# Cutting the token tiles of a fused attention and two-layer kernel along the batches

## The chip, the cores and the metric

The kernel runs on one core of a Trainium2 chip. The metric is the device time of one execution in microseconds; lower is better.

## The reference

```python
def _attn_ref(q, k, v, f):                   # q, k, v: (8, 8, 576, 64); f: (8, 8, 576)
    scores = scale * np.matmul(q, k.transpose(0, 1, 3, 2))
    log_f = np.log(np.clip(f, 0.0001, 1.0))
    cum = np.cumsum(log_f, axis=-1)
    decay = cum[:, :, :, None] - cum[:, :, None, :]
    scores = np.where(causal, -1000000000.0, scores + decay)
    ...                                      # softmax
    return np.matmul(attn, v)
def _moe_ref(x, w_in, w_out):                # x: (4608, 512); w_in: (512, 2048)
    h = x @ w_in
    relu6 = np.clip(h + 3.0, 0.0, 6.0)
    g = h * relu6 / 6.0
    return g @ w_out
x = attn_out.transpose(0, 2, 1, 3).reshape(B * S, H * D)
```

Causal attention with a decay is computed for 8 batches of 8 heads, 576 positions each. Its output, 4608 rows of 512, goes through two dense layers with a hard swish between them.

## The kernel before

**Attention.** A list of 68 steps `v`: 4 of kind A and 8 of kind B make batch 0, and 56 of kind F (steps 12 to 67) are one head each of batches 1 to 7. A step F computes scores on TensorE (`pn`, two halves, lines 608 and 611), takes row maxima on VectorE (619), exponentials (631) and a 16-bit cast (645) on ScalarE, a remainder on VectorE or GpSimd (648, 654), turns the result by DMA transposes (`pT<-ring`, 666) and multiplies it with V (`pav`, lines 691 to 696). All operands of the two layers are split into two 16-bit parts, a high and a low one, so each product there is three matmuls.

**Hand-over.** When two heads are done, their 128 columns of `x` are split into `xhl`, and `x_move` (755) turns them by DMA transposes into `xT`, the tile buffer from which the first layer reads. These, like all transfers of the attention part, are issued on SP's queue. There are three `xT` buffers of 512 rows; buffer 2 also holds raw V of batch 0 at the start (`v0`).

**Two layers.** Rows are cut into 9 tiles of 512. Since a batch has 576 rows, tile `t` (1 to 7) holds the last `64 t` rows of batch `t-1` and the first `512 - 64 t` of batch `t`; its `x` comes in runs of 64 rows. `h_unit` makes 128 of the 2048 hidden columns for the tile: 12 matmuls into an accumulator `ph` (lines 781 to 783), a Relu on ScalarE for each batch in the tile (791, since the scale is per batch), a multiply on VectorE (794), a cast on ScalarE (795) and a subtraction on VectorE (796), which fill `gT`. `out_unit` makes 128 output rows: 48 matmuls (803 to 805), a scaled copy on ScalarE (814), one transfer out (815). A tile has 16 first-layer and 4 output units; tile 0 is done in two halves of 256 rows. Accumulators of both kinds rotate over three slots.

**Order.** The units of a tile are put in a list once the last heads of its batch are handed over, so tiles 7 and 8 after the last head. `fill` is called eight times a step; each call adds a rate to a credit, and units are emitted while there is credit: `H_COST` twice for a first-layer unit, some 64 in all for a tile. The rate is `F_RATE`: 0.6 for batch 0, 0.45 for batch 1, 1.02 after. From this emission order a scheduler sets, when the program is built, the fixed order of the instructions on each engine; a later instruction can pass an earlier one there that it expects to wait. On the chip each engine then runs its list in order.

Of the kernel before, what the change touches and what calls it, by code (L numbers as in the profile page):

```python
# [15 lines left out]
ALU = mybir.AluOpType  # L16
# [4 lines left out]
def kernel(  # L21
# [32 lines left out]
    cpool = ctx.enter_context(tc.tile_pool(name="cpool", bufs=1))  # L54
    p2 = ctx.enter_context(tc.tile_pool(name="p2", bufs=2))
# [22 lines left out]
        out=W[:, 4 * P:], in_=W[:, 4 * P:], pattern=[[-1, P]],  # L78
# [16 lines left out]
    QA = 256  # L95
    CA = QA // P
# [21 lines left out]
    def init_qk(i, eng):  # L118
# [11 lines left out]
    VR = H * (D + 1)  # L130
# [21 lines left out]
    SV, IV, UO, UX, A1 = 0, 8, 16, 24, 32  # L152
# [47 lines left out]
    def scol(c):  # L200
        return SC[:, c:c + 1]
# [172 lines left out]
    def moe_scale_in(b, j):  # L374
        nc.vector.scalar_tensor_tensor(
            scol(A1 + NG * b + j), scol(IV + b), CG, scol(I1 + j), op0=ALU.mult, op1=ALU.mult
        )

    def moe_scale_out(b):
        nc.vector.scalar_tensor_tensor(  # L380
            scol(UO + b), scol(IV + b), 1.0 / (6.0 * CG), scol(I1R), op0=ALU.mult, op1=ALU.mult
        )
# [195 lines left out]
    for half in NAT:  # L578
        g = [0]
# [3 lines left out]
    o = 0  # L583
# [155 lines left out]
    def x_move(v):  # L739

        kind, n = VH[v]
        g = n if kind == "A" else n // 2
        b, cc = divmod(g, NPAIR)
        xhl = xpair[g][1]
        c0, c1 = {"A": (0, CA), "B": (CA, NCH), "F": (0, NCH)}[kind]

        if kind == "F":
            runs = [(0, 0, 1, 0), (0, 1, NCH, 1), (64, 1, NCH, 2)]
        else:
            runs = [(r * 64, c0, min(c1, NCH - r), r + 2 * c0) for r in range(2)]  # L750
        for r, c, last, u in runs:
            while c < last:
                t, q = divmod(S // 64 * b + u, TT // 64)
                k = min(last - c, (TT // 64 - q + 1) // 2)
                nc.sync.dma_start_transpose(
                    xT[t % 3][:, cc, q % 2, q // 2:q // 2 + k].rearrange("p c a t -> p (c a) t"),
                    xhl[r:r + 64, c:c + k].rearrange("p c a e -> p (c a e)"),
                )
# [13 lines left out]
    def h_unit(t, fc, c0, c1):  # L772
        x = xT[t % 3]
        nw = c1 - c0
        ph = mm_tile(f"ph_{t}_{fc}_{c0}", t > 0 or c0 > 0)[:, :nw]
        fs_ = slice(fc * P, (fc + 1) * P)
        for cc in range(NCC):
            xh, xl = (
                x[:, cc, :, c0 // P:c1 // P, hl].rearrange("p h c t -> p c h t") for hl in range(2)
            )  # L780
            nc.tensor.matmul(ph, w1[0][:, cc, fs_], xh, start=(cc == 0), stop=False)  # L781
            nc.tensor.matmul(ph, w1[0][:, cc, fs_], xl, start=False, stop=False)  # L782
            nc.tensor.matmul(ph, w1[1][:, cc, fs_], xh, start=False, stop=(cc == NCC - 1))  # L783
            if cc == 1 and nw == TT:
                yield H_COST
        r = p2.tile([P, TT], F32, tag="rt", name=f"r_{t}_{fc}_{c0}", bufs=3)[:, :nw]
        segs = [(0, nw, min(t, B - 1))]
        if 0 < t < B:
            segs = [(0, 64 * t, t - 1), (64 * t, TT, t)]
        for a, e, b in segs:  # L790
            nc.scalar.activation(  # L791
                r[:, a:e], ph[:, a:e], AF.Relu, bias=bias_r, scale=scol(A1 + NG * b + fc * NG // NFC)
            )
        nc.vector.scalar_tensor_tensor(r, r, 6.0 * CG, ph, op0=ALU.min, op1=ALU.mult)  # L794
        nc.scalar.copy(gT[:, 0, fc, c0:c1], r)  # L795
        nc.vector.tensor_tensor(gT[:, 1, fc, c0:c1], r, gT[:, 0, fc, c0:c1], op=ALU.subtract)  # L796
        yield H_COST

    def out_unit(t, s):
        po = mm_tile(f"po_{t}_{s}", t > 0 or s * P >= QA)  # L800
        ts_ = slice(s * P, (s + 1) * P)
        for fc in range(NFC):
            nc.tensor.matmul(po, gT[:, 0, fc, ts_], w2[:, fc, 0, :], start=(fc == 0), stop=False)  # L803
            nc.tensor.matmul(po, gT[:, 0, fc, ts_], w2[:, fc, 1, :], start=False, stop=False)  # L804
            nc.tensor.matmul(po, gT[:, 1, fc, ts_], w2[:, fc, 0, :], start=False, stop=(fc == NFC - 1))  # L805
            if fc % 2 and fc < NFC - 1:
                yield 2.0 - H_COST
        g = t * 4 + s
        b = (g * P) // S
        col = UO + b  # L810
        if (g * P + P - 1) // S != b:
            col = UX + b + 1
        o = p2.tile([P, DM], F32, tag="o", name=f"o_{t}_{s}")
        nc.scalar.activation(o, po, AF.Copy, scale=scol(col))  # L814
        nc.sync.dma_start(out[g * P:(g + 1) * P, :], o)
# [61 lines left out]
    units = []  # L877
# [36 lines left out]
    for i, (kind, n) in enumerate(VH):  # L914
        b, h = divmod(n, H)
        if kind == "A":
            b = h = 0
        wn = W_RATE["ABF".index(kind)]
        rates[0] = F_RATE[0] if kind == "B" else F_RATE[min(b, 2)]
        ahead = i + 2 < NV  # L920
# [99 lines left out]
```

## Time and profile before

| | |
|---|---|
| median of 3 runs | 1087.07 us (1083.17 to 1088.06) |
| profiled execution | 1083.28 us, span 1081.5 us |
| mean granted TensorE clock | 0.982 of full speed |
| busy: TensorE, VectorE, ScalarE, GpSimd | 93%, 67%, 56%, 38% |
| HBM read, written | 47.93 MB, 9.73 MB |
| DMA engines busy | 54.7% by the main queue |
| `x` hand-over | 148 DMA transposes |

The span runs from the first to the last instruction of the program; the execution's own time is 1.8 us longer. Groups of instructions are named by line, engine, operation and tile, with the count behind an x, then busy us and mean ns of one, then the idle time just before them with the instruction that ended it. A matmul's duration includes its way through the array, so consecutive ones overlap, and what a stream costs is read from the distance of the starts.

### The profile page before, as it was taken

What the parts mean: (1) busy time and instruction counts of PE and PEld (TensorE: products, weight loads), DVE (VectorE), ACT (ScalarE), POOL (GpSimd) and SP (SyncE); (2) the same over time, 40 slices, a digit from 0 to 9 for tenths busy, and PEclk for the clock granted to TensorE, in tenths of its full rate; (3) what the DMA queues carried; (4) which work ended last, traced back from release to release, by engine and by line L of the source; (5) the groups of instructions that cost most, each with busy time, mean ns of one, the idle gap of its engine ahead of it and who ended that gap; (6) DMA issues with size and microseconds to landing.
All of it is one profiled execution on the core that took longest, in us unless ns stands there. A gap on an engine that the chain in (4) does not pass through costs nothing.

```text
span 1081.5 us, 20281 instructions
## 1 busy us (share of the span) xinstructions
PE 1010.1 (93%) x7074; PEld 577.4 (53%) x7074; DVE 719.7 (67%) x1887; ACT 610.1 (56%) x1285; POOL 413.1 (38%) x505
## 2 busy tenths in 40 slices
PE   2799977988999999999999989999999999999998
PEld 2567854755555555555555545555555555444443
DVE  7869899876885688468865795689668841510520
ACT  4778656845764577356754674477447841621520
POOL 7344455335434445444544444454445420000000
PEclk9989989999999999999999999999999999999999
DMA  8866547767756666667576856675666651000001
GB/s 258 277 172 194 150 105 134 179 127 150 156 114 141 140 146 118 137 129 164 108 139 138 164 113 130 146 166 114 128 140 128 106 112 46 1 10 30 1 1 39
DMA packets 261650, 133.74 MB, mean 124 GB/s; under 512 B 229444, under 2 KB 231036, under 8 KB 261548
## 3 DMA queue, kind: packets, MB, share of 16 engines
q1 hardware_dynamic: 261548, 132.45, 54.7%
q8 instruction: 56, 0.92, 0.3%
q14 instruction: 46, 0.38, 0.1%
HBM read 47.93 MB, written 9.73 MB: 53 GB/s over the span
## 4 chain that ended last, share of the span: by engine, by line
PE 64%; DVE 12%; DMA 9%; issue 5%; ACT 5%; SPq 2%; POOL 2%; DVEq 0%; POOLq 0%; ACTq 0%
PE po L803 10%; PE po L804 10%; PE po L805 10%; PE ph L781 7%; PE ph L782 7%; PE ph L783 7%; DMA vst<-in_vS_dram 3%; PE pn L611 3%; PE pn L608 2%; DVE pp L619 2%; DVE ring L648 2%; DMA T<-TK 1%; DVE gT L796 1%; DMA w<-in_w_in_dram 1%; DVE r L794 1%
## 5 line engine op out<-in xcount | busy, mean ns | idle before, releaser
L781 PE MATMUL ph<-xT,w 128*128 128x512 f16 (+1 forms) x640 | 231.2, 363 | 14.5 <-DVE r L794 9.1
L782 PE MATMUL ph<-xT,w 128*128 128x512 f16 (+1 forms) x640 | 230.2, 363 | 0.0
L783 PE MATMUL ph<-xT,w 128*128 128x512 f16 (+1 forms) x640 | 230.0, 363 | 0.0
L631 ACT ACTIVATE pp<-pp,nb 128x192 f32<-128x192 f32 x280 | 138.5, 552 | 148.8 <-DVE nb L625 145.8
L804 PE MATMUL po<-w,gT 128*128 128x512 f16 x576 | 216.3, 381 | 6.1 <-DVE w L294 6.1
L805 PE MATMUL po<-w,gT 128*128 128x512 f16 x576 | 215.9, 381 | 0.0
L803 PE MATMUL po<-w,gT 128*128 128x512 f16 x576 | 213.6, 381 | 1.1 <-ACT o L814 0.8
L648 DVE TENSOR_TENSOR ring<-pp,ring 128x128 f16<-128x128 f32 (+2 forms) x216 | 131.5, 622 | 84.1 <-ACT ring L645 83.2
L791 ACT ACTIVATE r<-ph,bias_r,SC 128x256 f32<-128x256 f32 (+7 forms) x272 | 144.4, 570 | 28.6 <-PE ph L783 27.9
L794 DVE SCALAR_TENSOR_TENSOR r<-r,ph 128x512 f32<-128x512 f32 (+1 forms) x160 | 100.1, 627 | 88.9 <-ACT r L791 88.6
L458 POOL TENSOR_TENSOR T<-ST,T 64x576 fp32r<-64x576 f32 (+1 forms) x68 | 101.2, 1488 | 143.2 <-DMA T<-TK 133.4
L619 DVE CUSTOM_DVE_ANT_0 pp<-pn,W 128x192 f32<-128x192 f32 x280 | 122.9, 482 | 20.6 <-PE pn L611 16.6
L796 DVE TENSOR_TENSOR gT<-r,gT 128x512 f16<-128x512 f32 (+1 forms) x160 | 118.3, 743 | 27.4 <-ACT gT L795 26.6
L795 ACT CAST gT<-r 128x512 f16<-128x512 f32 (+1 forms) x160 | 91.8, 575 | 75.9 <-DVE r L794 75.8
L608 PE MATMUL pn<-TK,TQ 68*128 68x192 f32 x336 | 124.1, 383 | 5.8 <-issue 5.0
L611 PE MATMUL pn<-T,T 128*128 128x192 f32 x336 | 113.5, 368 | 4.3 <-POOL T L458 4.3
L645 ACT CAST ring<-pp 128x192 f16<-128x192 f32 x280 | 112.9, 452 | 0.0
L455 POOL TENSOR_TENSOR T<-ST,TQ 64x576 fp32r<-64x576 f32 (+2 forms) x68 | 97.6, 1435 | 24.8 <-PE pn L611 18.2
L654 POOL TENSOR_TENSOR ring<-pp,ring 128x128 f16<-128x128 f32 x96 | 61.5, 641 | 105.5 <-ACT ring L645 83.7
L782 PEld LDWEIGHTS <-w 128*128 128x128 f16 x640 | 62.7, 99 | 65.8 <-issue 20.9
L805 PEld LDWEIGHTS <-gT 128*128 128x128 f16 x576 | 56.8, 99 | 74.9 <-issue 13.7
L781 PEld LDWEIGHTS <-w 128*128 128x128 f16 x640 | 63.1, 99 | 62.2 <-issue 14.3
(136 smaller groups left out, 1703.4 us busy)
## 6 DMA issues: line engine op xcount, KB each, us to landing
ST<-in_qk_dram SPq DMA_DIRECT2D x64, 288.0 KB
T<-TK SPq DMA_DIRECT2D x64, 144.0 KB
out_dram<-o SPq DMA_DIRECT2D x36, 256.0 KB
ring<-in_w_out_dram SPq DMA_DIRECT2D x16, 512.0 KB
T<-TQ SPq DMA_DIRECT2D x56, 144.0 KB
vst<-in_vS_dram SPq DMA_DIRECT2D x7, 1040.0 KB
ring<-in_w_in_dram SPq DMA_DIRECT2D x9, 512.0 KB
w<-in_w_in_dram SPq DMA_DIRECT2D x7, 512.0 KB
```

Of the source, the lines that this page charges most:

```text
L608: nc.tensor.matmul(dst, TQ[i][0:D + 4, qs], TK[i][0:D + 4, a:e], start=True, stop=False)
L611: nc.tensor.matmul(dst, T7[j][:, qs], T1[j][:, a:e], start=False, stop=True)
L619: nc.vector.tensor_tensor_reduce(pp[:r, w:w + kw], pn[:r, o:o + kw], W[:r, 4 * P + r - kw:4 * P + r], 1.0, -3.0e38, ALU.add, ALU.max, accu ...
L631: nc.scalar.activation(x_, x_, AF.Exp, bias=nb[:r, e0 + x:e0 + x + 1], scale=0.125)
L648: eng.tensor_tensor(hl[:r, a:a + c * P], pp[:r, at[c] + 64:at[c] + kw], hl[:r, h0[c] + 64:h0[c] + kw], op=ALU.subtract,)
L781: nc.tensor.matmul(ph, w1[0][:, cc, fs_], xh, start=(cc == 0), stop=False)
L782: nc.tensor.matmul(ph, w1[0][:, cc, fs_], xl, start=False, stop=False)
L783: nc.tensor.matmul(ph, w1[1][:, cc, fs_], xh, start=False, stop=(cc == NCC - 1))
L791: nc.scalar.activation(r[:, a:e], ph[:, a:e], AF.Relu, bias=bias_r, scale=scol(A1 + NG * b + fc * NG // NFC))
L803: nc.tensor.matmul(po, gT[:, 0, fc, ts_], w2[:, fc, 0, :], start=(fc == 0), stop=False)
L804: nc.tensor.matmul(po, gT[:, 0, fc, ts_], w2[:, fc, 1, :], start=False, stop=False)
L805: nc.tensor.matmul(po, gT[:, 1, fc, ts_], w2[:, fc, 0, :], start=False, stop=(fc == NFC - 1))
```

## The change

Each batch now has one tile of its first (batch 0) or last 512 rows. The 64 rows left over of each two batches form a short unit of 128 rows, `moe_rest(k)`, put in the list behind the tile of every odd batch. Of the three `xT` buffers two alternate between the batches, and the third holds the four short units; it has room for all of them. The raw V of batch 0 moves to buffer 1. The rate of the later batches goes from 1.02 to 1.06, and a small first-layer unit costs half of `H_COST`, once.

```diff
-    F_RATE = (0.6, 0.45, 1.02)
+    F_RATE = (0.6, 0.45, 1.06)
-    xT = [cpool.tile([P, NCC, 2, TT // P, 2, 64], F16, name=f"xT{i}") for i in range(3)]
+    xT = [cpool.tile([P, NCC, TT // P, 2, P], F16, name=f"xT{i}") for i in range(3)]
...
# x_move
-        if kind == "F":
-            runs = [(0, 0, 1, 0), (0, 1, NCH, 1), (64, 1, NCH, 2)]
-        else:
-            runs = [(r * 64, c0, min(c1, NCH - r), r + 2 * c0) for r in range(2)]
-        for r, c, last, u in runs:
-            while c < last:
-                t, q = divmod(S // 64 * b + u, TT // 64)
-                k = min(last - c, (TT // 64 - q + 1) // 2)
-                nc.sync.dma_start_transpose(
-                    xT[t % 3][:, cc, q % 2, q // 2:q // 2 + k].rearrange("p c a t -> p (c a) t"),
-                    xhl[r:r + 64, c:c + k].rearrange("p c a e -> p (c a e)"),
-                )
-                c += k
-                u += 2 * k
+        c0, c1, rest = {"A": (0, CA, None), "B": (CA, NCH - 1, NCH - 1), "F": (1, NCH, 0)}[kind]
+        o = c0 - (1 if kind == "F" else 0)
+        if rest is not None:
+            nc.sync.dma_start_transpose(
+                xT[2][:, cc, b // 2, :, 64 * (b % 2):64 * (b % 2) + 64],
+                xhl[0:64, rest].rearrange("p a e -> p (a e)"),
+            )
+        nc.sync.dma_start_transpose(
+            xT[b % 2][:, cc, o:o + c1 - c0].rearrange("p c a t -> p (c a) t"),
+            xhl[:, c0:c1].rearrange("p c a e -> p (c a e)"),
+        )
...
# h_unit: segs comes from the caller; gT is written from column 0 for a short unit
-        segs = [(0, nw, min(t, B - 1))]
-        if 0 < t < B:
-            segs = [(0, 64 * t, t - 1), (64 * t, TT, t)]
-        yield H_COST
+        yield H_COST if nw >= TT // 2 else H_COST / 2
...
# out_unit
-        nc.sync.dma_start(out[g * P:(g + 1) * P, :], o)
+        p = 0
+        for r0, r1 in rows:
+            nc.sync.dma_start(out[r0:r1, :], o[p:p + r1 - r0])
+            p += r1 - r0
...
+    def moe_rest(k):
+        b = 2 * k
+        for fc in range(NFC):
+            yield from h_unit(
+                xT[2], fc, k * P, (k + 1) * P, [(0, 64, b), (64, P, b + 1)], True, f"r{k}"
+            )
+        r = S - 64 if b == 0 else S * b
+        yield from out_unit(0, UX + b + 1, [(r, r + 64), (S * (b + 1), S * (b + 1) + 64)], True, f"r{k}")
...
# done(v)
-            if b == B - 1:
-                units.append(one(B))
+            if b % 2:
+                units.append(moe_rest(b // 2))
```

Line numbers of the changed kernel differ from those above: 755 becomes 749 and 753, 781 to 783 become 775 to 777, 791 is 782, 795 is 787, 803 is 798, and attention's move by one.

In the built programs this looks as follows. SP's queue at the hand-over of one pair of heads of batch 2, before: `xT2` and `xT0` are tile buffers, `xhl_20` the pair's `x`, the last number the place in the program.

```order
L666 DMA_TRANSPOSE pT_22_3118<-ring0_123 128x12x128
L755 DMA_TRANSPOSE xT2_119<-xhl_20_3098 128x2x64
L755 DMA_TRANSPOSE xT2_119<-xhl_20_3098 128x6x64
L755 DMA_TRANSPOSE xT0_117<-xhl_20_3098 128x2x64
L755 DMA_TRANSPOSE xT2_119<-xhl_20_3098 128x4x64
L755 DMA_TRANSPOSE xT0_117<-xhl_20_3098 128x4x64
L417 DMA TK2_98<-decay_dram 2x576
```

The same pair after:

```order
L749 DMA_TRANSPOSE xT2_119<-xhl_20_3088 128x2x64
L753 DMA_TRANSPOSE xT0_117<-xhl_20_3088 128x8x128
```

Five issues became two. Next TensorE around the first short unit (`ph_r0`, `po_r0`), after; `pn_29` and `pn_33` are the scores of steps 29 and 33. Where its 16 small first-layer units begin:

```order
L609 MATMUL pn_29_0_4302<-TK2_98,TQ2_95 128x256
L612 MATMUL pn_29_0_4302<-T11_100,T71_102 128x256
L609 MATMUL pn_29_0_4302<-TK2_98,TQ2_95 64x64
L612 MATMUL pn_29_0_4302<-T11_100,T71_102 64x64
L775 LDWEIGHTS w10_113
L775 MATMUL ph_r0_0_0_4325<-xT2_119,w10_113 128x128
```

And where they end:

```order
L777 MATMUL ph_r0_15_0_4684<-xT2_119,w11_114 128x128
L609 MATMUL pn_33_0_5225<-TK0_96,TQ0_93 128x192
L612 MATMUL pn_33_0_5225<-T11_100,T71_102 128x192
L609 MATMUL pn_33_0_5225<-TK0_96,TQ0_93 128x320
L612 MATMUL pn_33_0_5225<-T11_100,T71_102 128x320
L609 MATMUL pn_33_0_5225<-TK0_96,TQ0_93 128x256
L612 MATMUL pn_33_0_5225<-T11_100,T71_102 128x256
L609 MATMUL pn_33_0_5225<-TK0_96,TQ0_93 64x64
L612 MATMUL pn_33_0_5225<-T11_100,T71_102 64x64
L798 LDWEIGHTS gT_116
L798 MATMUL po_r0_0_4731<-w2_115,gT_116 128x512
```

Between the two places stand 3.3 steps of scores and 3.0 steps of the product with V. The second short unit has steps 46 to 49 there, the third 63 to 66, again 3.3. In the program before, each full tile's 16 first-layer units had exactly four steps among them; after, tiles 1, 3 and 5 still have four, tile 2 has 1.3 of scores and 2.3 of products, tile 4 2.0 and 2.3, and tile 6 0.3 and 3.0. Before, at the end of tile 2 and the start of tile 3 (`pn_37` is step 37):

```order
L805 MATMUL po_2_3_5603<-w2_115,gT_116 128x512
L608 MATMUL pn_37_1_5748<-TK1_97,TQ1_94 128x320
L611 MATMUL pn_37_1_5748<-T11_100,T71_102 128x320
L608 MATMUL pn_37_1_5748<-TK1_97,TQ1_94 128x448
L611 MATMUL pn_37_1_5748<-T11_100,T71_102 128x448
L781 LDWEIGHTS w10_113
L781 MATMUL ph_3_0_0_5765<-xT0_117,w10_113 128x512
```

A full tile followed a full tile there; after, a short unit stands between them behind every odd one. Last, ScalarE's list among the small units of `r0`, after (`r` is the Relu's result, `gT` the first layer's, `pp` the exponentials):

```order
L787 CAST gT_116<-r_r0_5_0_4442 128x128
L782 ACTIVATE r_r0_6_0_4472<-ph_r0_6_0_4459,bias_r_86,SC_120 128x64 x2
L782 ACTIVATE r_r0_7_0_4491<-ph_r0_7_0_4478,bias_r_86,SC_120 128x64 x2
L632 ACTIVATE pp_30_0_4717<-pp_30_0_4717,nb_30_4707 128x192
L632 ACTIVATE pp_30_0_4717<-pp_30_0_4717,nb_30_4707 128x576
L632 ACTIVATE pp_30_0_4717<-pp_30_0_4717,nb_30_4707 64x64
L782 ACTIVATE r_r0_8_0_4512<-ph_r0_8_0_4499,bias_r_86,SC_120 128x64 x2
L787 CAST gT_116<-r_r0_6_0_4472 128x128
L646 CAST ring0_123<-pp_30_0_4717 128x192
```

And in tile 3, before:

```order
L791 ACTIVATE r_3_6_0_6077<-ph_3_6_0_6064,bias_r_86,SC_120 128x192
L791 ACTIVATE r_3_6_0_6077<-ph_3_6_0_6064,bias_r_86,SC_120 128x320
L631 ACTIVATE pp_39_0_6050<-pp_39_0_6050,nb_39_6040 128x192
L631 ACTIVATE pp_39_0_6050<-pp_39_0_6050,nb_39_6040 128x576
L631 ACTIVATE pp_39_0_6050<-pp_39_0_6050,nb_39_6040 64x64
L645 CAST ring0_123<-pp_39_0_6050 128x192
L795 CAST gT_116<-r_3_6_0_6077 128x512
```

Where one full unit stood beside a block of exponentials, three small ones stand now.

At the end of the program, before, tiles 7 and 8 follow the last head; after, tile 7 and the fourth short unit do, and all of tile 6's output units. Two of the short unit's 16 small units stand among tile 7's last output matmuls, the other 14 behind them.

More of the change, by code (lines that the diff above doesn't have):

```diff
@@ L47 @@
     TT = 512
-    NTILE = NT // TT
     VW = 2 * D + 1
@@ L135 @@
     gT = cpool.tile([P, 2, NFC, TT], F16, name="gT")
-    xT = [cpool.tile([P, NCC, 2, TT // P, 2, 64], F16, name=f"xT{i}") for i in range(3)]
+    xT = [cpool.tile([P, NCC, TT // P, 2, P], F16, name=f"xT{i}") for i in range(3)]
     v0 = [
         v16.bitcast(F32).rearrange("p n c j e -> p (n c j e)")[:, 0:3 * VR],
-        xT[2].bitcast(F32).rearrange("p a h c l t -> p (a h c l t)")[:, 0:2 * VR],
+        xT[1].bitcast(F32).rearrange("p a c l t -> p (a c l t)")[:, 0:2 * VR],
     ]
@@ L744, in x_move @@
         xhl = xpair[g][1]
-        c0, c1 = {"A": (0, CA), "B": (CA, NCH), "F": (0, NCH)}[kind]
-        if kind == "F":
-            runs = [(0, 0, 1, 0), (0, 1, NCH, 1), (64, 1, NCH, 2)]
-        else:
-            runs = [(r * 64, c0, min(c1, NCH - r), r + 2 * c0) for r in range(2)]
-        for r, c, last, u in runs:
-            while c < last:
-                t, q = divmod(S // 64 * b + u, TT // 64)
-                k = min(last - c, (TT // 64 - q + 1) // 2)
-                nc.sync.dma_start_transpose(
-                    xT[t % 3][:, cc, q % 2, q // 2:q // 2 + k].rearrange("p c a t -> p (c a) t"),
-                    xhl[r:r + 64, c:c + k].rearrange("p c a e -> p (c a e)"),
-                )
-                c += k
-                u += 2 * k
+        c0, c1, rest = {"A": (0, CA, None), "B": (CA, NCH - 1, NCH - 1), "F": (1, NCH, 0)}[kind]
[9 more added lines that the diff above has]
+        )
     turn = [0]
@@ L770, in mm_tile, with h_unit @@
         return ps_m.tile([P, TT], F32, tag="mm", name=name)
-    def h_unit(t, fc, c0, c1):
-        x = xT[t % 3]
+    def h_unit(x, fc, c0, c1, segs, three, name):
         nw = c1 - c0
-        ph = mm_tile(f"ph_{t}_{fc}_{c0}", t > 0 or c0 > 0)[:, :nw]
+        ph = mm_tile(f"ph_{name}_{fc}_{c0}", three)[:, :nw]
         fs_ = slice(fc * P, (fc + 1) * P)
         for cc in range(NCC):
-            xh, xl = (
-                x[:, cc, :, c0 // P:c1 // P, hl].rearrange("p h c t -> p c h t") for hl in range(2)
-            )
+            xh, xl = (x[:, cc, c0 // P:c1 // P, hl] for hl in range(2))
             nc.tensor.matmul(ph, w1[0][:, cc, fs_], xh, start=(cc == 0), stop=False)
@@ L785, in h_unit @@
                 yield H_COST
-        r = p2.tile([P, TT], F32, tag="rt", name=f"r_{t}_{fc}_{c0}", bufs=3)[:, :nw]
-        segs = [(0, nw, min(t, B - 1))]
-        if 0 < t < B:
-            segs = [(0, 64 * t, t - 1), (64 * t, TT, t)]
+        r = p2.tile([P, TT], F32, tag="rt", name=f"r_{name}_{fc}_{c0}", bufs=3)[:, :nw]
         for a, e, b in segs:
@@ L794, in h_unit, with out_unit @@
         nc.vector.scalar_tensor_tensor(r, r, 6.0 * CG, ph, op0=ALU.min, op1=ALU.mult)
-        nc.scalar.copy(gT[:, 0, fc, c0:c1], r)
-        nc.vector.tensor_tensor(gT[:, 1, fc, c0:c1], r, gT[:, 0, fc, c0:c1], op=ALU.subtract)
-        yield H_COST
-    def out_unit(t, s):
-        po = mm_tile(f"po_{t}_{s}", t > 0 or s * P >= QA)
+        g0 = c0 if x is not xT[2] else 0
+        nc.scalar.copy(gT[:, 0, fc, g0:g0 + nw], r)
+        nc.vector.tensor_tensor(
+            gT[:, 1, fc, g0:g0 + nw], r, gT[:, 0, fc, g0:g0 + nw], op=ALU.subtract
+        )
+        yield H_COST if nw >= TT // 2 else H_COST / 2
+    def out_unit(s, col, rows, three, name):
+        po = mm_tile(f"po_{name}_{s}", three)
         ts_ = slice(s * P, (s + 1) * P)
@@ L807, in out_unit, with moe_tile @@
                 yield 2.0 - H_COST
[L808 to L813, printed above, removed]
+        o = p2.tile([P, DM], F32, tag="o", name=f"o_{name}_{s}")
         nc.scalar.activation(o, po, AF.Copy, scale=scol(col))
-        nc.sync.dma_start(out[g * P:(g + 1) * P, :], o)
+        p = 0
+        for r0, r1 in rows:
+            nc.sync.dma_start(out[r0:r1, :], o[p:p + r1 - r0])
+            p += r1 - r0
         yield 2.0 - H_COST
-    def moe_tile(t, c0=0, c1=TT):
+    def moe_tile(b, c0=0, c1=TT):
         for fc in range(NFC):
             j, new = divmod(fc, NFC // NG)
-            if new == 0 and t < B and c0 == 0:
+            if new == 0 and c0 == 0:
                 while j not in w_in_done:
                     next(w_in_q, None)
-                moe_scale_in(t, j)
-            yield from h_unit(t, fc, c0, c1)
-        if t == 0:
+                moe_scale_in(b, j)
+            yield from h_unit(xT[b % 2], fc, c0, c1, [(0, c1 - c0, b)], b > 0 or c0 > 0, f"{b}")
+        if b == 0:
             for _ in wq:
                 pass
-        if t < B and c0 == 0:
-            moe_scale_out(t)
+        if c0 == 0:
+            moe_scale_out(b)
         for s in range(c0 // P, c1 // P):
-            yield from out_unit(t, s)
+            r = S * b + (64 if b else 0) + s * P
+            yield from out_unit(s, UO + b, [(r, r + P)], b > 0 or s * P >= QA, f"{b}")
+    def moe_rest(k):
[3 more added lines that the diff above has]
+                xT[2], fc, k * P, (k + 1) * P, [(0, 64, b), (64, P, b + 1)], True, f"r{k}"
+            )
+        r = S - 64 if b == 0 else S * b
+        yield from out_unit(0, UX + b + 1, [(r, r + 64), (S * (b + 1), S * (b + 1) + 64)], True, f"r{k}")
     dec = decay()
```

## The prediction

> **What bounds the kernel now.** I read the busy shares first, then the slices, the chain of waits, stretches of one kind of work, and last who waited for whom.
>
> ```profile
> PE 1010.1 (93%) x7074; PEld 577.4 (53%) x7074; DVE 719.7 (67%) x1887; ACT 610.1 (56%) x1285; POOL 413.1 (38%) x505
> PE   2799977988999999999999989999999999999998
> DVE  7869899876885688468865795689668841510520
> ACT  4778656845764577356754674477447841621520
> PEclk9989989999999999999999999999999999999999
> PE 64%; DVE 12%; DMA 9%; issue 5%; ACT 5%; SPq 2%; POOL 2%; DVEq 0%; POOLq 0%; ACTq 0%
> ```
>
> TensorE leads. Its idle time lies in the first slices; from the ninth on it is at 9 nearly throughout, with the clock at full. So the end is TensorE's work plus its idle time, and the change must be priced in both.
>
> ```profile
> core 0: us, PE busy (x) PEld busy (x) DVE busy (x) ACT busy (x) POOL busy (x), PEclk, DMA share, GB/s
> 390.00:432.00 42.00, 39.83 (x294) 21.76 (x293) 34.25 (x85) 29.00 (x63) 18.60 (x23) 0.96 0.67 141
> 432.00:485.00 53.00, 51.06 (x390) 28.01 (x388) 29.80 (x92) 24.34 (x54) 24.49 (x32) 1.00 0.65 131
> 903.00:944.00 41.00, 41.00 (x192) 18.58 (x191) 15.97 (x24) 19.99 (x38) 0.00 (x0) 1.00 0.08 21
> ```
>
> The first row is mostly a first-layer stretch beside attention: VectorE is busy 34 of 42 us, ScalarE 29, and TensorE has little cover left. The second is mostly second-layer units: the other two have slack. The third is after attention: TensorE without a gap, 192 matmuls of 512 columns in 41.0 us, 0.2135 us each.
>
> ```profile
> PE ph L781 <- DVE r L794: 9.1, 8, 3.2
> PE pav L691 <- DMA pT<-ring: 5.6, 4, 1.9
> PE ph L781 <- DMA xT<-xhl: 5.3, 4, 2.2
> ```
>
> These are waits of TensorE (us in total, times, longest) that the change can touch: 20 us together. More than that it can hardly win, because the other large ones belong to the start and to the weights.
>
> **Part 1: more, shorter matmuls.** One tile of 512 columns (192 first-layer matmuls) becomes four short units, 768 matmuls of 128 columns; the columns streamed are the same. The trace has no stream 128 wide, so I bound it by its neighbours.
>
> ```profile
> 893.10 0.19 PE L696 MATMUL pav<-v,pT 128*128 128x65 f16 x1
> ...
> 894.15 0.38 PE L803 MATMUL po<-w,gT 128*128 128x512 f16 x1
> 128.01 0.27 PE L782 MATMUL ph<-xT,w 128*128 128x256 f16 x1
> ...
> 129.10 0.27 PE L783 MATMUL ph<-xT,w 128*128 128x256 f16 x1
> ```
>
> The 34 attention matmuls from 893.10 to 894.15 are 64 or 65 columns wide, each with its own load of 128x128 weights, and follow each other every 0.031 us. Ten steps of 256 columns take 1.09 us, 0.109 each. Between them 128 columns come to 0.057 us. So 768 x 0.057 = 43.5 us against 192 x 0.2135 = 41.0: **+2.5 us**, and 10.9 us for each short unit's 192.
>
> The Trainium skill, "TensorE: Matmul & The Clock Gate", section "Back-to-back issue gap", says that a stream of weight load and matmul settles at about 81 ns for 128 columns. By that the term would be 768 x 0.081 - 41.0 = +21 us, an estimate from that page, and the sum 1116 rather than 1112: beside attention the longer matmuls would fill time in which TensorE waits anyway, and only the tail's 192 add 4.6 us. The 0.031 us rows with their own loads speak against it; no run here shows 128 columns themselves.
>
> **Part 2: what the short units ask of ScalarE and VectorE.** Each of the 64 small first-layer units has two Relu of 64 columns, one multiply, one cast and one subtraction of 128. The Relu count is 272 either way; multiplies, casts and subtractions go from 160 to 208.
>
> ```profile
> L791 ACT ACTIVATE r<-ph,bias_r,SC 128x64 f32<-128x64 f32 x32 | 12.7, 400 | 6.6 <-PE ph L783 6.6
> L791 ACT ACTIVATE r<-ph,bias_r,SC 128x448 f32<-128x448 f32 x32 | 22.9, 719 | 3.2 <-PE ph L783 3.2
> L645 ACT CAST ring<-pp 128x192 f16<-128x192 f32 x56 | 18.9, 338 | 0.0
> L645 ACT CAST ring<-pp 64x64 f16<-64x64 f32 x56 | 13.6, 242 | 0.0
> L794 DVE SCALAR_TENSOR_TENSOR r<-r,ph 128x256 f32<-128x256 f32 x32 | 12.9, 409 | 0.4 <-ACT r L791 0.2
> L648 DVE TENSOR_TENSOR ring<-pp,ring 128x128 f16<-128x128 f32 x56 | 22.6, 403 | 40.6 <-ACT ring L645 40.5
> L814 ACT ACTIVATE o<-po,SC 128x512 f32<-128x512 f32 x36 | 24.4, 683 | 100.1 <-PE po L805 98.3 <-DMA out_dram<-o 1.8
> 266.76 1.01 ACT L791 ACTIVATE r<-ph,bias_r,SC 128x64 f32<-128x64 f32 x2
> ```
>
> ScalarE: 2 x 0.400, and a cast of 128 columns between 0.242 and 0.338, 0.29: 1.09 us a unit. VectorE: at most 0.409 for the multiply and 0.403 for the subtraction, 0.81 us. TensorE needs 12 x 0.057 = 0.68 us. So while short units run, ScalarE is the slower one, where a full unit gives it 2.6 us of matmuls to hide under. Back to back, instructions overlap: the last row's pair of 64 and 448 columns takes 1.01 us against 0.400 + 0.719, a factor of 1.11.
>
> In the built order the 16 small units of one short unit stand among 3.3 steps of attention scores (from step 29 to 33 for the first), where before 16 full units stand among 4.0. A step's price:
>
> ```profile
> 367.04 0.39 PE L781 MATMUL ph<-xT,w 128*128 128x512 f16 x1
> 477.67 0.39 PE L781 MATMUL ph<-xT,w 128*128 128x512 f16 x1
> ```
>
> These are the first matmuls of tiles 2 and 3: a tile and eight steps take 110.6 us, 13.8 a step. Less 384 x 0.2135 = 82 us for the tile, attention costs TensorE (110.6 - 82)/8 = 3.6 us a step. The stretch 432 to 485 is 3.84 steps: ScalarE (24.34 - 4 x 0.683)/3.84 = 5.6 us a step, VectorE 29.80/3.84 = 7.8.
>
> One such window then asks for
> - TensorE: 10.9 + 3.2 x 3.6 = 22.4 us;
> - ScalarE: 16 x 1.09 + 3.3 x 5.6 = 36.0;
> - VectorE: 16 x 0.81 + 3.3 x 7.8 = 38.7.
>
> With the overlap of 1.11 VectorE and ScalarE need 34.9 and 32.4. TensorE may run ahead by three accumulators, about 3 x 1.09 = 3.3 us. It waits 34.9 - 3.3 - 22.4 = 9.2 us a window; three windows stand beside attention (the fourth short unit is in the tail): **+28 us**. No full unit stands in these windows to fill the hole. Bounds: with VectorE forgotten and ScalarE packed, 32.4 - 3.3 - 22.4 = 6.7, so 20 us; with attention at its old 13.8 us a step, 46 - 22.4 = 23.6, so 71 us. I stay near the low end because engine work limits, not a wait that the trace shows.
>
> **Part 3: the tail.** The last short unit follows the last full tile; its small units stand nearly all behind that tile's output matmuls, 14 of them with nothing else on TensorE: 14 x (1.09/1.11 - 0.68) = **+4.2 us** (none if the scheduler's few early ones suffice, 5.7 without overlap). Its output leaves in two transfers rather than one, **+0.5** (L815 below). The second layer's 1728 matmuls are unchanged.
>
> **Part 4: transposes on SP.**
>
> ```profile
> L755 SPq DMA_TRANSPOSE xT<-xhl x148: 1158/1238/2477, 41.0 to 906.1; - x148
> L666 SPq DMA_TRANSPOSE pT<-ring x112: 1276/1490/3870, 153.2 to 891.6; - x112
> 586.03 5.47 SPq L755 DMA_TRANSPOSE xT<-xhl  x4
> 591.60 0.52 SPq L815 DMA_DIRECT2D out_dram<-o  x1
> 592.17 1.21 SPq L755 DMA_TRANSPOSE xT<-xhl  x1
> 592.68 0.38 PE L781 MATMUL ph<-xT,w 128*128 128x512 f16 x1 [2.22 <-DMA xT<-xhl]
> ```
>
> A pair of heads hands over in five issues, 7.3 us of SP here, the first tile matmul that needs the data waiting 2.22. After: two issues. A 128-partition transpose costs like the larger pT ones, 1.49 us: 68 x 1.49 = 101 us of SP instead of 148 x 1.24 = 184. SP is not the bound, so only waits of TensorE count: of the 5.3 us for xT I take **-4.5**, also because at the new pace of 1.06 a full tile finds its predecessor unfinished from batch 3 on and starts late. The rows moved are the same, so the DMA engines gain nothing. Two x buffers in place of three make batch b+2's first transpose wait for tile b's last first-layer matmul; by the order that is done 1 to 2 steps ahead, so I cost it at zero. If it slips, SP holds the pT and T transfers behind it. The raw V of batch 0, now in buffer 1, is last read before batch 1 writes there: zero.
>
> **Part 5: full tiles.** One Relu instead of two a unit relieves ScalarE alone. Tiles 2, 4 and 6 come behind a window in which attention ran ahead, so their first layers have at most 2.3 scores steps beside them, not 4, and half of the 9.1 us for VectorE goes: **-4**.
>
> **Sum:** 2.5 + 28 + 4.2 + 0.5 - 4.5 - 4 = +26.7 on the profiled execution's 1083.28 us (span 1081.5), 1110. That execution is 3.8 us below the median of 1087.07; I put the forecast between, at **1112**.
>
> **Rivals.**
> (a) *The windows are covered* (faster). If the engines overlap so well that a window costs TensorE 1 us, what is left is 2.5 + 3 + 4.7 less the 20 us of waits that earlier data and a standing backlog remove: -10, 1074. For it: SP's relief is real. Against: 36 us of ScalarE over 22 of TensorE. It decides below (20 - 7.2)/3 = 4.3 us a window. Chance 0.10.
> (b) *Even*: windows near 5 us and the waits gone, within 0.5% (about what this measurement can tell from no change) of 1087. 0.10.
> (c) *Attention sets the windows' pace*, each small unit passing ScalarE and VectorE twice in queues that hold whole blocks of exponentials: 71 us instead of 28, 1155. Against: the loads above do not reach it. 0.10.
> My forecast has 0.70, with 1092 to 1140 as its own range. With (c) that makes 0.80 for slower, 0.10 each for the rest. The range 1086 to 1142 leaves out (a) and the upper half of (c).
>
> **What would show it.** Right: in three stretches of some 30 to 35 us, at the short units, TensorE's busy time falls to two thirds, its waits for the multiply and its Relu grow from 9 us to some 30, ScalarE and VectorE near full; TensorE waits again near the end, in the last short unit; the xT wait falls under 1 us; 128-column matmuls every 0.057 us. Wrong: TensorE at 9 there, or 128 columns at 0.08 us, or the waits for pT and T growing because SP is held.

## The result, and the profile after

The changed kernel takes 1113.49 us (median of 4 runs, 1109.88 to 1116.56), the one before 1085.49: a ratio of 1.0256 with a 95% interval of 1.0213 to 1.0299. The profiled execution takes 1112.34 us, its span is 1110.6, 29.1 more than before. Medians from here on are those of the fast runs; one slow run is left out by that, of e10, with 2074.38 us.

The page of the changed kernel, busy shares and slices:

```profile
PE 1023.8 (92%) x7650; PEld 613.6 (55%) x7650; DVE 739.7 (67%) x1983; ACT 619.8 (56%) x1333; POOL 399.6 (36%) x505
PE   2799977899999799999999899999999799999997
PEclk9989989999999889999999899999999999999999
```

TensorE has 7 or 8 in slices 13, 22 and 31 (counted from 0) where it had 9: near 365, 615 and 865 us, where the first three short units stand. In two of the places the granted clock dips too. Stretches from the first matmul of each short unit to its first output matmul, and the tail's from its first to its last small one:

```profile
core 0: us, PE busy (x) PEld busy (x) DVE busy (x) ACT busy (x) POOL busy (x), PEclk, DMA share, GB/s
363.40:400.40 37.00, 27.09 (x364) 25.55 (x362) 29.74 (x96) 28.31 (x83) 18.75 (x24) 0.82 0.64 134
616.40:648.80 32.40, 24.61 (x355) 22.52 (x354) 25.19 (x84) 24.87 (x74) 21.41 (x25) 0.89 0.77 165
864.80:899.30 34.50, 25.54 (x364) 23.86 (x362) 27.76 (x91) 26.64 (x78) 16.68 (x21) 0.90 0.62 110
1075.90:1095.00 19.10, 17.54 (x220) 13.59 (x219) 6.65 (x26) 12.31 (x43) 0.00 (x0) 1.00 0.05 16
```

The three windows last 37.0, 32.4 and 34.5 us. TensorE is recorded busy for some three quarters of them, so it is idle for 9.9, 7.8 and 9.0 us; ScalarE and VectorE are at 77 to 80%, not full. TensorE's waits after, to be held against the three of before and this fourth:

```profile
PE pn L608 <- issue: 5.0, 1, 5.0
```

After:

```profile
PE ph_r L775 <- DVE r_r L785: 18.3, 11, 5.8
PE pn L609 <- issue: 16.0, 5, 4.7
PE pav L692 <- DMA pT<-ring: 5.5, 8, 1.2
PE ph L775 <- DVE r L785: 4.6, 4, 2.3
PE ph L775 <- DMA xT<-xhl: 0.6, 1, 0.6
```

The first row is new: small units waiting for an accumulator that VectorE has not yet read. The waits for `xT` are nearly gone, those of full units for VectorE halved. In the three windows the waits are these (the first two rows are the first window's, the next two the second's, the last two the third's):

```profile
PE ph_r L775 <- DVE r_r L785: 8.7, 2, 5.8
PE pav L692 <- DMA pT<-ring: 1.2, 1, 1.2
PE pn L609 <- issue: 5.8, 2, 4.7
PE ph_r L775 <- DVE r_r L785: 1.5, 3, 0.6
PE ph_r L775 <- DVE r_r L785: 6.8, 2, 4.1
PE pav L692 <- DMA pT<-ring: 1.8, 2, 0.9
```

For the waits of a score matmul (`pn`) the profile names no releaser ("issue"). The longest of them, and what VectorE had just ended:

```profile
629.24 0.50 PE L609 MATMUL pn<-TK,TQ 68*128 68x192 f32 x1 [4.69 <-issue]
629.06 0.07 DVE L620 DVE_READ_ACCUMULATOR2_ANT MF<- 64x1 f32 x1
```

Score accumulators have two slots, one for each half of a step, so this matmul needs the slot whose row maxima VectorE finished at 629.13; its weights were loaded from 629.21 on. So here too TensorE waits for VectorE's list to get there, as far as the times tell.

### The profile page after: what moved, and what is told of

Same layout as the page of the kernel before. It is cut to its first block, busy times and chain, and to the rows that moved or that the text cites. A ratio compares the mean times of both kernels' runs of the same rounds, so it can differ in the third digit from the quotient of the medians.

```text
span 1110.6 us, 21517 instructions
## 1 busy us (share of the span) xinstructions
PE 1023.8 (92%) x7650; PEld 613.6 (55%) x7650; DVE 739.7 (67%) x1983; ACT 619.8 (56%) x1333; POOL 399.6 (36%) x505
## 4 chain that ended last, share of the span: by engine, by line
PE 73%; DMA 7%; DVE 7%; ACT 5%; issue 4%; POOL 2%; SPq 1%; POOLq 0%; DVEq 0%; ACTq 0%
PE po L798 9%; PE po L799 9%; PE po L800 9%; PE ph L775 9%; PE ph L777 8%; PE ph L776 8%; PE pn L609 3%; PE pn L612 3%; DMA pT<-ring 3%; DMA vst<-in_vS_dram 2%; PE pav L696 1%; DMA w<-in_w_in_dram 1%; PE po_r L798 1%; PE pav L697 1%; PE po_r L800 1%
## 5 line engine op out<-in xcount | busy, mean ns | idle before, releaser
L775 PE MATMUL ph<-xT,w 128*128 128x512 f16 (+1 forms) x576 | 201.0, 359 | 5.2 <-DVE r L785 4.6
L777 PE MATMUL ph<-xT,w 128*128 128x512 f16 (+1 forms) x576 | 200.2, 358 | 0.0
L776 PE MATMUL ph<-xT,w 128*128 128x512 f16 (+1 forms) x576 | 200.1, 357 | 0.0
L799 PE MATMUL po<-w,gT 128*128 128x512 f16 x512 | 191.9, 381 | 2.1 <-DVE w L295 2.1
L649 DVE TENSOR_TENSOR ring<-pp,ring 128x128 f16<-128x128 f32 (+2 forms) x216 | 139.1, 656 | 79.3 <-ACT ring L646 78.8
L800 PE MATMUL po<-w,gT 128*128 128x512 f16 x512 | 191.9, 381 | 0.0
L798 PE MATMUL po<-w,gT 128*128 128x512 f16 x512 | 189.7, 382 | 2.4 <-ACT o L804 1.6
L785 DVE SCALAR_TENSOR_TENSOR r<-r,ph 128x512 f32<-128x512 f32 (+1 forms) x144 | 89.3, 621 | 82.4 <-ACT r L782 81.9
L782 ACT ACTIVATE r<-ph,bias_r,SC 128x512 f32<-128x512 f32 (+1 forms) x144 | 104.0, 727 | 45.6 <-PE ph L777 41.4
L776 PEld LDWEIGHTS <-w 128*128 128x128 f16 x832 | 83.4, 101 | 73.5 <-issue 29.2
L787 ACT CAST gT<-r 128x512 f16<-128x512 f32 (+1 forms) x144 | 81.7, 568 | 73.7 <-DVE r L785 73.2
L788 DVE TENSOR_TENSOR gT<-r,gT 128x512 f16<-128x512 f32 (+1 forms) x144 | 100.4, 702 | 32.1 <-ACT gT L787 30.7
L777 PEld LDWEIGHTS <-w 128*128 128x128 f16 x832 | 83.4, 101 | 57.2 <-issue 5.1
L447 POOL TENSOR_SCALAR TK<-ST 64x576 fp32r<-64x576 f32 (+1 forms) x68 | 51.0, 749 | 169.9 <-PE pn L609 133.0
L775 PEld LDWEIGHTS <-w 128*128 128x128 f16 x832 | 82.5, 101 | 52.2 <-issue 8.9
L655 POOL TENSOR_TENSOR ring<-pp,ring 128x128 f16<-128x128 f32 x96 | 55.9, 583 | 133.8 <-ACT ring L646 95.3
```

The costliest lines, as they stand in the source:

```text
L649: eng.tensor_tensor(hl[:r, a:a + c * P], pp[:r, at[c] + 64:at[c] + kw], hl[:r, h0[c] + 64:h0[c] + kw], op=ALU.subtract,)
```

## The experiments

The changed kernel was not run again beside the experiments. The kernel before was, at medians of 1082 to 1084 us where it had 1085.49 beside the changed kernel. So a gain over the changed kernel is 3 to 6 us smaller by the ratios than by the times, and both are given where it matters.

**e1: the small instructions once for four blocks.** Four hidden blocks of a short unit go into one accumulator of 512 columns, and each elementwise instruction covers the four.

```diff
-        for fc in range(NFC):
-            yield from h_unit(xT[2], fc, k * P, (k + 1) * P, [(0, 64, b), (64, P, b + 1)], True, f"r{k}")
+        for j in range(NG):
+            yield from h_quad(k, j, [(0, 64, b), (64, P, b + 1)], f"r{k}")
...
+    def h_quad(k, j, segs, name):
+        ph = mm_tile(f"ph_{name}_{j}", True)
+        for i in range(4):
+            fc = 4 * j + i               # 12 matmuls into ph[:, i * P:(i + 1) * P]
...
+        p4, r4 = (t.rearrange("p (f t) -> p f t", f=4) for t in (ph, r))
+        for a, e, b in segs:             # Relu of r4[:, :, a:e] from p4[:, :, a:e]
...
+        nc.vector.scalar_tensor_tensor(r, r, 6.0 * CG, ph, op0=ALU.min, op1=ALU.mult)
+        gh, gl = (gT[:, hl, 4 * j:4 * j + 4, 0:P] for hl in range(2))
+        nc.scalar.copy(gh, r4)
+        nc.vector.tensor_tensor(gl, r4, gh, op=ALU.subtract)
```

> Changed kernel, but a short unit's first layer is made in 4 units of four hidden blocks (4 x 128 columns in one accumulator) in place of 16: the same matmuls of 128 columns, while Relu, multiply, cast and subtraction are done once for four blocks (2 + 1 + 1 + 1 instructions instead of four times that). Theory A (TensorE waits in the short units for the small instructions of ScalarE and VectorE): the three windows and the tail's wait go, some 28 and 4 us, so 1078 to 1086 us. Rival B (it is the matmuls of 128 columns, at 0.08 us or more, or what else the cut costs TensorE): the matmuls are all still there, so at least 1105. Rival C (backlog and rate, or the two x buffers): unchanged, 1108 to 1116.

Measured: 1082.7 us, ratio to the kernel before 1.0004 (0.9976 to 1.0031). The whole loss is gone, with every matmul of 128 columns still there: rivals B and C fall. The same stretches:

```profile
364.30:378.50 14.20, 14.20 (x248) 13.58 (x247) 11.04 (x26) 8.89 (x20) 6.72 (x8) 1.00 0.71 136
604.50:618.90 14.40, 14.36 (x248) 13.62 (x247) 10.60 (x25) 9.96 (x22) 5.91 (x8) 1.00 0.72 141
841.30:852.90 11.60, 11.60 (x216) 11.21 (x215) 8.99 (x20) 7.28 (x17) 6.10 (x7) 1.00 0.76 119
```

TensorE is full there at full clock. But the built order changed with the edit as well: it puts 1.0 steps of scores between the short unit's first matmuls (0.3 in the third stretch as cut here), not 3.3. So e1 shows that the small instructions, with the order that the scheduler makes of them, are the cause, not yet by which way.

**e2: four small units share an accumulator**, elementwise work still done for each of the 16 apart.

```diff
+        for i in range(4):               # in h_quad, in place of the instructions over four blocks
+            d = ph[:, i * P:(i + 1) * P]
...
+            nc.vector.scalar_tensor_tensor(r, r, 6.0 * CG, d, op0=ALU.min, op1=ALU.mult)
+            nc.scalar.copy(gT[:, 0, fc, 0:P], r)
+            nc.vector.tensor_tensor(gT[:, 1, fc, 0:P], r, gT[:, 0, fc, 0:P], op=ALU.subtract)
```

> Changed kernel, but four small units share one accumulator (so TensorE may run 12 of them ahead, not 3), with Relu, multiply, cast and subtraction still done for each of the 16 apart. Theory A1 (the load of ScalarE and VectorE, about 36 and 39 us a window by durations, sets the window): the load is the same, TensorE must wait for it at the output unit, so 1100 to 1113 us. Theory A2 (the round trip of each small unit through two engines, with only three accumulators, sets it): the wait goes, 1080 to 1092. Rivals B and C: unchanged, 1108 to 1116.

Measured: 1110.64 us, 1.0275 (1.0253 to 1.0297). That is 3 us less than the changed kernel by the times and no less by the ratios: more room to run ahead gives next to nothing. TensorE finishes the first short unit's small matmuls 15 us after they begin (363.5 to 378.8) and then has attention alone until its first output matmul at 391.3; 7.55 us of that it is idle before a score matmul. The lack of accumulators is not the cause.

**e3: another place.** The same instructions, the 16 small units emitted one by one among the second to fourth output units of the odd full tile.

```diff
+        side = rest_h(b // 2) if b % 2 else iter(())
         for s in range(c0 // P, c1 // P):
-            yield from out_unit(...)
+            for c in out_unit(...):
+                yield c
+                if s > c0 // P:          # one small first-layer unit after each piece
+                    c = next(side, 0)
...
```

> Changed kernel with the same instructions, but a short unit's 16 first-layer units are emitted one by one among the second to fourth output units of the odd full tile ahead of it, where ScalarE and VectorE have slack, and no longer in a block behind it. Theory A: the windows shrink to little, 1083 to 1098 us. Rival B (price of the matmuls themselves) and C (rate, buffers): 1108 to 1116.

Measured: 1103.56 us, 1.0221 (1.0191 to 1.0251): 10 us better than in a block by the times, 4 by the ratios, whose intervals overlap; so a gain is not certain, and it is short of the 1083 to 1098 expected. Slack of ScalarE and VectorE beside output units covers a small part at most.

**e4: the rate back at 1.02.**

```diff
-    F_RATE = (0.6, 0.45, 1.06)
+    F_RATE = (0.6, 0.45, 1.02)
```

> Changed kernel with the rate of the later batches back at 1.02. Theory A: the windows stay, with a little less of the two layers emitted before the end, 1110 to 1120 us. Rival C (the loss comes from emitting the two layers faster, 1.06): back to 1085 to 1095.

Measured: 1121.78 us, 1.0381 (1.0364 to 1.0398). The rate of 1.06 does not cause the loss; without it the change is worse, by 2 us more than I expected. Why so much was not followed up.

**e5 and e6: fewer small instructions.** e5 has one Relu of 128 columns where there were two of 64, e6 no subtraction for the small units.

```diff
# e5 (leaves out the second batch's own scale)
-                xT[2], fc, k * P, (k + 1) * P, [(0, 64, b), (64, P, b + 1)], True, f"r{k}"
+                xT[2], fc, k * P, (k + 1) * P, [(0, P, b)], True, f"r{k}"
# e6 (leaves out the low part of the short units' hidden values)
-        nc.vector.tensor_tensor(
+        if nw > P:
+            nc.vector.tensor_tensor(
...
```

> Changed kernel with one Relu of 128 columns in each small unit in place of two of 64 (it leaves out the second batch's own scale). 16 ScalarE instructions fewer in each window, 0.30 to 0.40 us each. If ScalarE's load sets the windows: 16 x 0.3 to 0.4 x 3 = 14 to 19 us less, and some 4 in the tail, 1092 to 1099 us. If VectorE sets them alone: the windows stay, only the tail gains, 1108 to 1114. If the round trip through both does: a part, 1098 to 1108.

> Changed kernel without the subtraction on VectorE in the small units (it leaves out the low part of the short units' hidden values; the matmuls that read it stay). 16 VectorE instructions fewer in each window, 0.43 us each, and the scaled cast ends each unit. If VectorE's load sets the windows: 16 x 0.3 to 0.43 x 3 = 14 to 20 us less, 1091 to 1099 us. If ScalarE's load alone does: 1108 to 1114. If the round trip through both: a part, 1098 to 1108.

Measured: e5 1102.26 us, 1.0182 (1.0156 to 1.0209); e6 1107.7, 1.0234 (1.0204 to 1.0264). One saves 11 us by the times and 8 by the ratios; the other 6 and 2, which the ratios' intervals don't tell apart from nothing. Neither comes to the 14 us or more that were expected if one engine's load alone set the windows.

**e10: both of these**, three small instructions in place of five.

> Changed kernel with one Relu per small unit and without the subtraction (leaves out the second batch's own scale and the low part of the short units' hidden values): a small unit has three small instructions, not five. One Relu alone gave 11 us, no subtraction alone 6. If the round trip of both engines sets the windows, the two add up to 17 or more: 1089 to 1097 us. If one engine's load hid the other's gain: 1085 to 1089. If attention beside them is the floor: no less than 1100.

Measured: 1098.77 us (1097.36 to 1102.72), 1.0159 (1.0111 to 1.0208): 15 us less by the times, 10 by the ratios. That is about the sum of e5's and e6's gains. It lies between the 1089 to 1097 that I gave for a round trip and the 1100 that I gave for a floor set by attention, 1.2 us below the latter, and so decides between neither. Its stretches:

```profile
364.30:395.70 31.40, 26.01 (x322) 24.08 (x320) 24.21 (x79) 21.69 (x60) 17.07 (x22) 0.79 0.65 133
613.20:642.20 29.00, 22.93 (x356) 21.20 (x355) 19.94 (x68) 22.63 (x63) 17.89 (x22) 0.94 0.77 146
858.10:887.00 28.90, 24.27 (x355) 22.68 (x354) 21.84 (x74) 21.94 (x62) 16.35 (x21) 0.89 0.73 128
```

The score matmuls alone (line 609, six a step) in the same stretches, TensorE and its weight loads:

```profile
364.30:395.70 31.40, 7.46 (x21) 4.45 (x20) 0.79 0.65 133
613.20:642.20 29.00, 6.21 (x21) 3.64 (x20) 0.94 0.77 146
858.10:887.00 28.90, 6.28 (x21) 3.64 (x20) 0.89 0.73 128
```

Each engine is idle for about a sixth of the time or more, and the windows last 29 to 31 us all the same. One of the 21 matmuls began before the stretch, as in the counts further down, so each holds 20/6 = 3.3 steps: 9.4, 8.7 and 8.7 us a step.

**e9: the small units' matmuls twice.**

```diff
-        for cc in range(NCC):
+        for cc in list(range(NCC)) * (2 if nw == P else 1):
```

> Changed kernel with the first-layer matmuls of the small units done twice (the second pass overwrites the first): 768 matmuls of 128 columns more, 43.5 us of TensorE at 0.057 us each, nothing added on ScalarE and VectorE. Theory A (beside attention TensorE waits for the other two anyway): most of the 33 us in the three windows is hidden, and in the tail 16 x 1.36 us takes the place of 19, so some 3 to 6 us there; 1113 to 1128 us. Rival B (TensorE's matmuls set the windows, at 0.057 us or more): 1150 to 1165. Rival D (the clock's half-speed spells, which follow TensorE's idling, make the windows long): the spells in the windows go and with them 5 to 10 us, so 1103 to 1115.

Measured: 1146.3 us, 1.059 (1.0552 to 1.0628): 33 us more, where A expected up to 15 and B 37 or more, so neither range holds. Its stretches:

```profile
364.60:409.70 45.10, 37.57 (x607) 35.44 (x606) 38.57 (x123) 32.77 (x94) 28.10 (x35) 0.98 0.71 151
622.80:667.70 44.90, 37.94 (x560) 36.27 (x559) 35.14 (x108) 30.07 (x87) 24.41 (x32) 0.88 0.87 166
883.30:923.50 40.20, 35.52 (x600) 33.49 (x599) 29.79 (x115) 30.90 (x90) 20.00 (x24) 1.00 0.62 123
1097.10:1131.60 34.50, 28.14 (x413) 24.30 (x412) 7.00 (x28) 13.59 (x46) 0.00 (x0) 1.00 0.03 9
```

The score matmuls alone in the first three:

```profile
364.60:409.70 45.10, 9.07 (x31) 5.42 (x30) 0.98 0.71 151
622.80:667.70 44.90, 8.50 (x27) 5.22 (x26) 0.88 0.87 166
883.30:923.50 40.20, 7.97 (x27) 4.73 (x26) 1.00 0.62 123
```

The windows grew by 8.1, 12.5 and 5.7 us, 26.3 together, for 31.7 us of matmuls; TensorE's idle time in them fell only from 26.7 to 19.2 us. Again the windows are long by the steps in them: the scheduler now put 30/6, 26/6 and 26/6 there, 9.0, 10.4 and 9.3 us each. So the hole was not free room: what is added to the small units makes the order put more attention beside them. Rival D's forecast fails: the clock is at or near full in two of the windows, and the program got longer, not shorter. The tail's stretch grew by 15.4 us: 10.6 are the 192 matmuls more, and most of the rest is that TensorE waits there four times for VectorE's multiply, 1.6 us each, where its waits in the changed kernel's stretch come to 1.6 us. Why it waits more there is not shown.

**e11: the kernel before at rate 1.06.**

> The kernel before with the later rate at 1.06 alone. Its tiles of 64 units of credit were already emitted as fast as they came at 1.02, so theory A: 1080 to 1087 us, no change. Rival C (a faster rate costs attention): 1090 or more.

Measured: 1087.5 us, 1.0046 (1.0019 to 1.0073). The rate alone costs the old kernel about half a percent, at the upper edge of the 1080 to 1087 expected by A and short of C's 1090.

**e7, e8, e12: variants of e1.** e7 has the rate 1.125 with e1, e8 puts each short unit ahead of the odd full tile, e12 does both.

```diff
# e7, e12
-    F_RATE = (0.6, 0.45, 1.06)
+    F_RATE = (0.6, 0.45, 1.125)
# e8, e12 (the scales of the odd batch are set in the short unit then)
+            if b % 2:
+                units.append(moe_rest(b // 2))
             units.append(one(b, QA if b == 0 else 0, TT))
-            if b % 2:
-                units.append(moe_rest(b // 2))
```

> The kernel with four hidden blocks in each unit of the short units, with the later rate at 1.125, which is what eight steps need for a tile and half a short unit (72 of credit). Theory A: nothing waits for the rate once the windows are gone, so like the one at 1.06, 1078 to 1085 us; less backlog at the end means a shorter tail but a longer stretch beside attention. Rival C (a faster rate starves attention): 1085 to 1095.

> The kernel with four hidden blocks in each unit of the short units, with each short unit ahead of the odd full tile and no longer behind it, so that the program ends with full output units. In the profile of the one behind, TensorE waits 3.3 and 2.5 us in the last short unit; these should go where the full tile's first units can fill them: 1075 to 1081 us. If the full tile cannot start before the short unit's output is done (it overwrites the same hidden values), the wait only moves: 1079 to 1086.

> Four hidden blocks in each unit of the short units, the short unit ahead of the odd tile, and the later rate 1.125. The first two together took 1079 us, three below the kernel before, at the edge of what was resolved; a higher rate brings the first layer of tile 7 beside the last attention: 1075 to 1080 if that helps, 1080 to 1086 if the tail's work only moves.

Measured: e7 1082.01 us, 1.0 (0.9978 to 1.0023); e8 1079.32, 0.9982 (0.996 to 1.0004), not told apart from the kernel before; e12 1073.11, **0.9912 (0.9881 to 0.9943)**, which beats both kernels and lies below the 1075 to 1080 expected. Its four stretches:

```profile
254.20:270.80 16.60, 13.68 (x235) 12.98 (x235) 14.14 (x39) 10.97 (x25) 11.23 (x13) 1.00 0.70 131
490.90:504.20 13.30, 13.30 (x222) 12.33 (x221) 9.27 (x24) 7.72 (x17) 5.87 (x8) 1.00 0.58 129
724.90:738.20 13.30, 13.30 (x222) 12.33 (x221) 8.60 (x24) 7.72 (x17) 6.11 (x8) 1.00 0.70 129
940.70:967.70 27.00, 27.00 (x289) 18.16 (x288) 3.95 (x8) 5.90 (x11) 0.00 (x0) 1.00 0.11 32
```

TensorE is full in all but the first, the last short unit included, since the last full tile's units fill it. That both edits are needed together was measured; why one alone gives so little was not.

## Why the prediction was right

Forecast 1112 us, measured 1113.5. By terms, on the spans (29.1 us):

- **Part 1, +2.5.** From 370.99 to 371.32 the small matmuls of the first window follow each other:

```profile
370.99 0.22 PE L776 MATMUL ph_r<-xT,w 128*128 128x128 f16 x1
...
371.32 0.22 PE L776 MATMUL ph_r<-xT,w 128*128 128x128 f16 x1
```

  Six steps take 0.33 us, 0.055 each at full clock; 768 of them 42 us in place of 41: about +1. e1, with the same matmuls and no holes in its windows, has TensorE busy 2.5 us longer than the kernel before, 1012.6 against 1010.1. The Trainium skill's 81 ns for such a stream ("TensorE: Matmul & The Clock Gate", "Back-to-back issue gap") does not hold here; the figure of about 56 ns that the same section gives for a matmul by itself does.
- **Part 2, +28 in the windows.** TensorE is idle in them for 26.7 us, against 9.2 us forecast for each. Sign and size of the waiting were right. But TensorE is also recorded busy there for 77.2 us, not for three times the prediction's 22.4, so the windows last 36.7 us more than those 67.2. Up to the first output matmul two of them hold 4.0 steps of scores, not 3.3, which is attention moved there and no loss by itself; and part of the work ran at a lower clock. The waits for the multiply grew from 9.1 to 23.4 us, where some 30 were forecast.
- **Part 3, +4.2 in the tail.** 19.1 us hold 192 small and 28 full matmuls, 10.6 + 6.0 us: +2.5.
- **Part 4, -4.5.** The `xT` wait went from 5.3 to 0.6: -4.7. The waits for pT, which a held SP would lengthen, did not grow: 5.5 us against 5.6.
- **Part 5, -4.** Full units' waits for VectorE went from 9.1 to 4.6: -4.5.

Taken over the whole program, TensorE's idle time grew by 15.4 us (from 71.4 to 86.8) and its busy time by 13.7 (from 1010.1 to 1023.8). The prediction had 24 for the first and 2.5 for the second. It put nothing down for the clock: in stretches of half a microsecond, TensorE's busy time times the share of the clock that was missing adds up to 23.9 us here, 14.3 before and 13.5 in e1, so some 10 us of TensorE's longer busy time come with a lower clock. On the other side, idle time outside the windows shrank by 11.3 us and not by the 4 that parts 3 to 5 make: by the 4.7 and 4.5 above, and by small waits that were not followed up, while the tail's stretch has only 1.6 us of idle time. That the total came out within 2 us is thus in part luck.

The step that does not hold is the reason given in part 2: that the loads of VectorE and ScalarE limit, which should be "near full". They were at 77 to 80%. By that reckoning most of e9's matmuls should have vanished in the hole, but of the 33 us only 15 lie in the tail, so more than half of the 31.7 us in the windows was not hidden. e10 does not speak against it: with some 5 us less ScalarE and 6.9 less VectorE work a window it should have gained 15 to 21 us over three windows and come to 1093 to 1098, and it took 1098.8. What the waits show instead is that TensorE waits for instructions to have their turn in the lists of VectorE and ScalarE, the multiply of a small unit for the most part and, as far as the times tell, the row maxima of a step, while neither engine is full. VectorE in its turn stood idle for 48.1 us before the small multiplies, waiting for the Relu:

```profile
L785 DVE SCALAR_TENSOR_TENSOR r_r<-r_r,ph_r 128x128 f32<-128x128 f32 x64 | 17.3, 277 | 49.5 <-ACT r_r L782 48.1 <-PE ph_r L777 1.2
```

This lies nearer to rival (c). The windows of the changed kernel, e9 and e10 last 8.6 to 10.4 us for each step of attention that the built order put into them. The score matmuls of the changed kernel's windows:

```profile
363.40:400.40 37.00, 8.51 (x25) 5.38 (x24) 0.82 0.64 134
616.40:648.80 32.40, 6.85 (x21) 4.10 (x20) 0.89 0.77 165
864.80:899.30 34.50, 7.67 (x25) 4.77 (x24) 0.90 0.62 110
```

Without the one that began before each stretch these are 24/6, 20/6 and 24/6 steps, so 9.3, 9.7 and 8.6 us each, while a step and its share of small units give TensorE some 6.5 us. Rival (c) had the pace at the old 13.8 us, which was too slow. That this pace is a floor of attention is not shown: before, from 251 to 264 us, two steps went by in 13.0 us, 6.5 each. And e3, with full output units among its windows, still lost 20 us. So the small instructions act in two ways, by holding up the engines and by making the scheduler put attention where full units' matmuls should be; no run holds the order still while the instructions change, and how much each way costs stays open.

## What to carry to other kernels

When a tile is cut to get round an awkward boundary, count the instructions that every piece needs on each engine, not the columns: here the matmuls cost some 2 us more, and the small instructions behind them nearly 30. Where pieces share a scale, gather several in one accumulator and do the elementwise work once; this gave the whole loss back, and together with the short unit put ahead of a full one and a higher rate it made a kernel 0.9% faster than before. In a program whose order is fixed when it is built, count also what stands among the new units in that order, since here a scheduler that held small units back brought other work forward that could not keep the first engine busy.

## What the runs showed of the hardware

TensorE's clock fell in the windows: the granted clock was 0.82, 0.89 and 0.90 in them, and 1.00 in the same places of e1. After the first window's wait of 5.83 us the small matmuls start 0.11 us apart, twice the 0.055 of before:

```profile
377.42 0.26 PE L775 MATMUL ph_r<-xT,w 128*128 128x128 f16 x1 [5.83 <-DVE r_r L785]
377.48 0.31 PE L776 MATMUL ph_r<-xT,w 128*128 128x128 f16 x1
377.59 0.31 PE L777 MATMUL ph_r<-xT,w 128*128 128x128 f16 x1
377.69 0.31 PE L775 MATMUL ph_r<-xT,w 128*128 128x128 f16 x1
```

So in these windows the starved TensorE was also a slow one for a while; by the reckoning above, 11.7 us of its busy time in the three windows are lost to that. The windows don't need it to be long, since e9's first and third were with clocks of 0.98 and 1.00; what they would last in the changed kernel at full clock was not tried. And just ahead of that wait VectorE's instructions took longer than usual, while GpSimd worked (the first two rows are VectorE's, the others GpSimd's, some left out between):

```profile
372.94 2.12 DVE L788 TENSOR_TENSOR gT<-r_r,gT 128x128 f16<-128x128 f32 x3
374.98 2.19 DVE L649 TENSOR_TENSOR ring<-pp,ring 128x256 f16<-128x256 f32 x2
...
372.74 1.53 POOL L459 TENSOR_TENSOR T<-ST,T 64x576 fp32r<-64x576 f32 x1
...
375.29 1.47 POOL L459 TENSOR_TENSOR T<-ST,T 64x576 fp32r<-64x576 f32 x1
```

Three subtractions of 128 columns take 2.12 us, 0.71 each, where the mean over this kernel is 0.425; two of 256 take 2.19, 1.10 each, where it is 0.598:

```profile
L788 DVE TENSOR_TENSOR gT<-r_r,gT 128x128 f16<-128x128 f32 x64 | 25.6, 425 | 3.9 <-ACT gT L787 3.9
L649 DVE TENSOR_TENSOR ring<-pp,ring 128x256 f16<-128x256 f32 x56 | 33.5, 598 | 28.1 <-ACT ring L646 28.0
```

In those 4.2 us GpSimd is at work nearly all the time, twice with its own subtraction of 576 columns. That the one slows the other was not tried. The Trainium skill ("SBUF — State Buffer", "SBUF: two separate sides") has a VectorE operation with two inputs in SBUF and a GpSimd operation that reads SBUF take turns at a shared port; these rows agree with that, and no run here tells it from another cause.
